# A linear-attention and two-MoE kernel on one core: a new table of steps for the parts, loads and sums of the chunks, with the diagonals and products dealt anew among the engines

## The chip, the cores and the metric

The kernel runs on one core of a Trainium2 chip. The metric is the device time of one execution in microseconds; the kernel before took 535.35 us (median of three runs, 534.69 to 539.89). TensorE (PE) does matmuls and transposes, VectorE (DVE) and GpSimd (POOL) elementwise work, scans and reductions, ScalarE (ACT) activations and copies, and SyncE (SP) issues the DMAs. Each engine works through its own instructions in a fixed order; an instruction waits until what it reads is written and until its buffer is free.

## What is computed

An attention with a decaying state, then a MoE with a clipped gate, then a soft MoE over 32 slots:

```python
for t in range(S):                       # attention, B=4, H=8, S=768, D=48
    cur = np.einsum('bhd,bhe->bhde', u[None] * kt, vt)
    y[:, :, t] = np.einsum('bhd,bhde->bhe', rt, state + cur)
    state = wt[:, :, :, None] * state + np.einsum('bhd,bhe->bhde', kt, vt)
...
h = x @ w_in                             # x: 3072 x 384, w_in: 384 x 2048
g = h * np.clip(h + 3.0, 0.0, 6.0) / 6.0
x = g @ w_out                            # back to 384
...
logits = x @ phi                         # 32 slots, 8 experts
d = softmax(logits, over tokens)
slot_input = d.T @ x
slot_out = relu(slot_input[e] @ w1[e]) @ w2[e]
return softmax(logits, over slots) @ slot_out
```

## The kernel before, in words

**Chunks.** The 3072 tokens are 24 chunks g of 128 tokens, six for each batch. For each chunk two loads are issued on SP: wkr (w, k and r by head pairs, L234) and rkv (r, k and v by tokens, L243). Its parts, with the names used in the tables, are: pw, a scan that gives the running decay e, with a reciprocal and a copy pt on ACT (L250, L252, L254); pv, a second scan (L260); pk and pq, products of k and r with the decays, on DVE or POOL (L263, L270); pg, two squares on ACT that feed a range guard (L267); rk and ru, the products r times k and times u by tokens (L276, L280), and pc, their sum (L284); d0 and d1, two halves of the diagonals of the score matrix, four heads each, on ACT as four activations (L293) or on POOL as one product (L295); sm and sc, the scores and their copy into the masked triangle (L306, L311); kt, the transposed keys (L222, copied at L322); y, the chunk's output (L373, L377, copies L394 and L395); tm and tu, the state's update (L333, L346 to L349).

**Steps.** Three chunks form a block m of 384 tokens. When a block's y is complete, six DMAs on SP rearrange it (L400), and ax splits it into a high and a low part (L419 on ACT; L420 on DVE, or on POOL for blocks 2 and 4). Each block then has 16 steps, 128 in all. Step s does nine matmuls h (L498) into one of three PSUM banks, relu on ACT (L501) and g on DVE (L502, which frees the bank). Two steps later g is transposed: on DVE (L529), whence four DMAs take each group of four steps to DRAM (L518) and one brings it back (L519), or on PE (L222, copied at L540 or L542) at the start and the end. l are the logits' matmuls of four steps (L551). r_logits of a block (rl) splits the logits into two parts (L570 on ACT, L571 on DVE), sums them on PE (L573; L576 and L577 for the last block), takes the minimum (L583, L585) and exponentials (L590, L591, L593); r_back (rb) transposes them (L605), and r_acc (ra) adds the slot inputs into acc (L643, L646). After step 127 follow the experts, from L729 on.

**What sets the order.** The program is written out token by token. START lists the tokens before step 0 by hand. After that every token has a step: a chunk's base step is 16(m-1) plus an entry of YB, each part has a fixed distance from it (pw, pv and rk five steps earlier, sm and sc at it, and so on), and the table LATER shifts single tokens by some steps; PLACES does the same for the loads and splits of the first MoE's weights. Within a step h comes first, then the transposes, l, and the other tokens in order of their entry. A scheduler then places the instructions engine by engine from this sequence, so a shifted token moves its instructions on all engines and its DMAs on SP. The lists RKD, RUD, PKD and PQD name the chunks whose rk, ru, pk or pq run on DVE instead of POOL, DGA the halves whose diagonals run on ACT.

## Time and profile before

| | |
|---|---|
| median of three runs | 535.35 us (534.69 to 539.89) |
| the profiled execution | 535.26 us |
| its span in the trace | 533.5 us, 1.76 us outside it |
| PE busy | 474.5 us, 89% |
| DVE busy | 366.4 us, 69% |
| ACT busy | 237.5 us, 45% |
| POOL busy | 153.0 us, 29% |
| costliest group | h, L498: 1152 matmuls, 232.2 us |
| mean granted TensorE clock | 0.941 |

A row of the timeline gives the start of an instruction or of a run of like ones (x9), its duration, engine, line, operation and tiles; in square brackets stands how long the engine had been idle before it and what ended that idle time. The matmuls of PE overlap, so the duration of one is longer than the distance to the next.

### The profile page before, as it was taken

The page shows a single profiled execution, that of the slowest core. Times are in us where ns is not written, and L with a number is a line of the kernel's source. Part 1 is how long each engine was busy: PE and PEld are TensorE (multiplying, and loading weights), DVE is VectorE, ACT ScalarE, POOL GpSimd, SP SyncE. Part 2 cuts the span into 40 slices and gives each one's busy share as a digit, 9 for nine tenths or more (in the row PEclk, how much of TensorE's full clock was granted, in tenths as well). Part 3 has the DMA queues.
Part 4 walks back from the last instruction along what each step waited for, and adds up shares of the span by engine and source line. Part 5 has one row for each costly group of instructions (what it writes and reads, how often), then busy time and mean ns, then how long its engine had stood idle before and what let it go on. Part 6 is the DMA issues. An engine that isn't in the chain of part 4 may idle for free.

```text
span 533.5 us, 10165 instructions
## 1 busy us (share of the span) xinstructions
PE 474.5 (89%) x3934; PEld 375.0 (70%) x3934; DVE 366.4 (69%) x669; ACT 237.5 (45%) x580; POOL 153.0 (29%) x150
## 2 busy tenths in 40 slices
...
GB/s 297 413 280 123 88 122 183 259 86 70 107 3 109 1 121 109 184 192 279 268 120 249 326 224 145 286 222 197 119 329 199 377 315 336 419 324 270 398 172 232
DMA packets 40263, 114.13 MB, mean 214 GB/s; under 512 B 4464, under 2 KB 22928, under 8 KB 40208
## 3 DMA queue, kind: packets, MB, share of 16 engines
...
q8 instruction: 33, 0.54, 0.4%
...
## 4 chain that ended last, share of the span: by engine, by line
PE 45%; DVE 15%; DMA 9%; ACT 4%; issue 2%; POOL 2%; SPq 1%; POOLq 0%; DVEq 0%; ACTq 0%
PE h L498 22%; DMA rkv<-in_rkv_dram 4%; DMA wkr<-in_wkr_dram 4%; PE lps L551 3%; PE rot L222 3%; PE sides L643 3%; DVE g L502 2%; DVE wkr L260 2%; PE rot L799 2%; DVE e L250 2%; PE rot L373 2%; DVE gsq L529 2%; PE rot L377 2%; PE sides L306 1%; PE po L851 1%
## 5 line engine op out<-in xcount | busy, mean ns | idle before, releaser
L498 PE MATMUL h<-x,wt 128*128 128x384 f32 x1152 | 232.2, 349 | 21.6 <-DVE g L502 11.0
L498 PEld LDWEIGHTS h<-x,wt 128*128 128x128 f32 x1152 | 201.1, 192 | 43.6 <-DVE g L502 15.0
L501 ACT ACTIVATE g<-h,half 128x384 f32<-128x384 f32 x128 | 71.9, 575 | 62.6 <-PE h L498 57.7
L502 DVE SCALAR_TENSOR_TENSOR g<-g,h 128x384 f32<-128x384 f32 x128 | 68.7, 542 | 39.6 <-ACT g L501 36.0
L529 DVE STREAM_TRANSPOSE gsq<-g 128x384 f32<-128x384 f32 x88 | 49.6, 569 | 4.1 <-DMA via<-gsq 2.9
L250 DVE TENSOR_TENSOR_SCAN e<-wkr,d1r 128x516 f32<-128x516 f32 x24 | 32.3, 1351 | 23.2 <-DMA wkr<-in_wkr_dram 23.1
L295 POOL TENSOR_TENSOR att<-cst,cd 128x512 f32<-128x512 f32 x32 | 37.0, 1169 | 27.1 <-DVE cd L284 21.7
L270 POOL TENSOR_TENSOR wkr<-wkr 128x512 f32<-128x512 f32 x18 | 23.9, 1328 | 64.3 <-DVE wkr L260 35.9
L311 DVE COPY_PREDICATED att<-upm,sides 128x512 f32<-128x512 uint32 x48 | 32.1, 721 | 11.3 <-POOL att L295 5.7
L377 PE MATMUL rot<-att,rkv 128*64 128x128 f32 x384 | 32.5, 297 | 7.0 <-DVE att L311 7.0
L260 DVE TENSOR_TENSOR_SCAN wkr<-wkr,d1f 128x516 f32<-128x516 f32 x24 | 35.4, 1475 | 0.1
L377 PEld LDWEIGHTS rot<-att,rkv 128*64 128x64 f32 x384 | 25.0, 147 | 13.9 <-DVE att L311 8.2
L306 PE MATMUL sides<-wkr 64*128 64x128 f32 x384 | 31.6, 302 | 3.2 <-DVE wkr L270 1.2
L263 POOL TENSOR_TENSOR wkr<-wkr,e 128x512 f32<-128x512 f32 x16 | 20.9, 1309 | 44.2 <-DVE e L250 38.2
L306 PEld LDWEIGHTS sides<-wkr 64*128 64x128 f32 x384 | 26.0, 202 | 8.5 <-issue 4.3
L551 PE MATMUL lps<-g,ws 128*32 128x384 f32 x256 | 29.2, 519 | 1.2 <-DVE g L502 1.2
L293 ACT ACTIVATE att<-cst,cd 128x128 f32<-128x128 f32 x64 | 20.3, 393 | 16.5 <-DVE cd L284 16.5
L267 ACT ACTIVATE wkr<-wkr 128x516 f32<-128x516 f32 x24 | 15.2, 633 | 26.1 <-POOL wkr L270 15.6
L349 POOL TENSOR_TENSOR st<-sm,pt 128x192 f32<-128x192 f32 x20 | 13.8, 688 | 43.4 <-DVE sm L348 22.3
L280 POOL TENSOR_TENSOR rkv<-rkv,u_b 128x384 f32<-128x384 f32 x18 | 19.5, 1081 | 21.9 <-DVE rkv L276 9.2
L722 POOL COPY c<-chi 128x128 f32<-128x128 f32 x6 | 2.2, 364 | 78.7 <-DVE chi L720 40.9
L373 PE MATMUL rot<-wkr,st 64*64 64x128 f32 x320 | 24.5, 291 | 0.0
...
## 6 DMA issues: line engine op xcount, KB each, us to landing
...
```

Source lines behind the costliest of these rows:

```text
L250: nc.vector.tensor_tensor_scan(out=flat(e)[:, ::-1], data0=behind.pop(g)[:, ::-1], data1=flat(d1r)[:, ::-1], initial=0.0, op0=ALU.mult, op ...
L260: nc.vector.tensor_tensor_scan(out=fw, data0=fw, data1=fd, initial=0.0, op0=ALU.mult, op1=ALU.add)
L295: nc.gpsimd.tensor_tensor(out=att[g][:, hs, :], in0=ident.unsqueeze(1).to_broadcast([128, 4, C]), in1=cd[g][:, hs].unsqueeze(2).to_broadca ...
L306: nc.tensor.matmul(out=sps[g][:, x, p * C:(p + 1) * C], lhsT=kt_[hs, p, :], rhs=qt_[hs, p, :])
L311: nc.vector.copy_predicated(out=att[g][:, x::2, :], mask=upm.unsqueeze(1).to_broadcast([128, NP, C]), data=ps[:, x].rearrange("p (a t) -> ...
L373: nc.tensor.matmul(out=ps[hs, k * C:(k + 1) * C], lhsT=stl[g][hs, p, :], rhs=qt_[hs, p, :], start=(k == 0), stop=False)
L377: nc.tensor.matmul(out=ps[64 * x:64 * x + 64, k * C:(k + 1) * C], lhsT=vt[:, 2 * p + x, :], rhs=a[:, 2 * p + x, :], start=(first and k == ...
L498: mm = nc.tensor.matmul(out=ps, lhsT=a[:, wp, f % 2, kt * 128:(kt + 1) * 128], rhs=x_[:, xp, kt, :], start=(kt == 0 and i == 0), stop=(kt ...
L501: ra = nc.scalar.activation(out=t, in_=ps, func=ACTF.Relu, scale=1.0 / 6.0, bias=half)
L502: sv = nc.vector.scalar_tensor_tensor(out=t, in0=t, scalar=1.0, in1=ps, op0=ALU.min, op1=ALU.mult)
L529: nc.vector.transpose(out=gsq[m, q][:, :, :, i, :].rearrange("p r j c -> p j r c"), in_=gt[s].rearrange("p (j r c) -> p j r c", j=n, r=4))
L551: mm = nc.tensor.matmul(out=lps[m][32 * i:32 * i + 32, :], lhsT=wsl[q][:, i, :], rhs=gt.pop(NF * m + 4 * q + i), start=(q == 0), stop=(q = ...
```

## The change

Only tables of numbers differ; every part of every chunk is still computed. Of the halves in DGA, seven go from POOL to ACT (chunks 6, 9, 15: first half; 12, 22: second; 10: both) and two come back ((8, 1), (20, 0)). PQD gains pq of chunks 10, 11, 20 and 23 for DVE and loses 13; RKD gains 8 and loses 0 and 14; RUD gains 10 and 20 and loses 8 and 17. YB moves three chunks' base steps by one or two. LATER has other shifts for most tokens, START another order of its tokens, and of PLACES the first four entries change places.

```diff
-RKD = (0, 2, 4, 7, 9, 10, 11, 12, 14, 16, 17, 19, 23)
-RUD = (4, 8, 12, 17, 18, 21)
+RKD = (2, 4, 7, 8, 9, 10, 11, 12, 16, 17, 19, 23)
+RUD = (4, 10, 12, 18, 20, 21)
 PKD = (2, 4, 8, 9, 10, 11, 12, 17)
-PQD = (0, 2, 3, 7, 13, 19)
+PQD = (0, 2, 3, 7, 10, 11, 19, 20, 23)
...
-DGA = ((0, 0), (0, 1), (1, 1), (2, 0), (6, 1), (7, 0), (8, 0), (8, 1), (11, 1), (13, 1), (14, 1), (16, 1), (18, 0), (19, 0), (20, 0), (21, 0))
+DGA = ((0, 0), (0, 1), (1, 1), (2, 0), (6, 0), (6, 1), (7, 0), (8, 0), (9, 0), (10, 0), (10, 1), (11, 1), (12, 1), (13, 1), (14, 1), (15, 0), (16, 1), (18, 0), (19, 0), (21, 0), (22, 1))
...
-YB = ((-5, 3, 5), (0, 4, 8), (-6, -2, 4), (-7, -3, 2), (-6, -2, 2), (-10, -8, -1), (-13, -7, -4))
+YB = ((-5, 3, 3), (0, 4, 8), (-6, -2, 4), (-7, -3, 1), (-6, -1, 2), (-10, -8, -1), (-13, -7, -4))
...
 LATER = {
-    'N7': -5, 'pw4': -1, 'rk7': -4, 'rl0': -1, 'sc8': 1, 'pg10': 1, 'N6': -1, 'tu7': 3, 's10': 2, 'pk13': -2, 'rb6': -1,
...
+    'N7': -5, 'pw4': -3, 'rk7': -2, 'rl0': -1, 'sc8': 2, 'N6': -2, 'tu7': 3, 's10': 2, 'pk13': -2, 'rb6': -1, 's01': 1, 'd18':
```

What this moves is seen in the engines' orders; three places follow, each before and after the change.

The first is ACT at steps 65 to 68. g_3174 is the relu of step 66 in the change (67 before), part is the split of block 3's logits, pt and e belong to the scans of chunks 19 and 20, att is the diagonal of chunk 18. Before:

```order
L254 ACTIVATE pt_3126<-e_3123 128x4
L570 ACTIVATE part_3149<-lps_2694 128x384
L267 ACTIVATE e_3123,guard_96<-e_3123 128x516
L501 ACTIVATE g_3139<-h_3129,half_95 128x384
L501 ACTIVATE g_3174<-h_3164,half_95 128x384
L267 ACTIVATE wkr_3069,guard_96<-wkr_3069 128x516
L293 ACTIVATE att_3180<-cst0_91,cd_3146 128x128 x4
L395 ACTIVATE y_2763<-rot_3098 128x3x128
L254 ACTIVATE pt_3332<-e_3329 128x4
L267 ACTIVATE e_3329,guard_96<-e_3329 128x516
L501 ACTIVATE g_3231<-h_3221,half_95 128x384
```

In the change:

```order
L570 ACTIVATE part_3149<-lps_2810 128x384
L254 ACTIVATE pt_3088<-e_3085 128x4
L501 ACTIVATE g_3174<-h_3164,half_95 128x384
L267 ACTIVATE e_3085,guard_96<-e_3085 128x516
L501 ACTIVATE g_3201<-h_3191,half_95 128x384
L501 ACTIVATE g_3246<-h_3236,half_95 128x384
L267 ACTIVATE wkr_3046,guard_96<-wkr_3046 128x516
L293 ACTIVATE att_3207<-cst0_91,cd_3205 128x128 x2
L590 ACTIVATE e2_3158,zb_3159<-rot_3148,mrun_104 128x384
L591 ACTIVATE al_3160<-mrun_104 128x1
L293 ACTIVATE att_3207<-cst0_91,cd_3205 128x128 x2
```

The split L570 has moved from behind pt of chunk 19 to ahead of it, and the relu of step 68 (g_3231 before, g_3246 now) from behind two squares, the diagonals, a y copy and chunk 20's pt to right behind the relu of step 67.

The second is DVE from g of step 67 (g_3174 before, g_3201 now) on; g of step 68 is g_3231 before and g_3246 now. Before:

```order
L502 SCALAR_TENSOR_TENSOR g_3174<-g_3174,h_3164 128x384
L394 COPY y3_2764<-rot_3098 128x128
L250 SCALAR_TENSOR_TENSOR e_3329<-wkr_3297,d1r_100 128x516
L583 TENSOR_REDUCE mx_3155<-rot_3148 128x1
L529 STREAM_TRANSPOSE gsq_3142<-g_3174 128x3x4x32
L252 RECIPROCAL d1f_99<-e_3329 128x4
L311 COPY_PREDICATED att_3180<-upm_92,sides_3186 128x4x128 x2
L585 TENSOR_TENSOR mrun_104<-mx_3155,mrun_104 128x1
L260 SCALAR_TENSOR_TENSOR wkr_3297<-wkr_3297,d1f_99 128x516
L276 TENSOR_TENSOR rkv_3178<-rkv_3178 128x384
L502 SCALAR_TENSOR_TENSOR g_3231<-g_3231,h_3221 128x384
L593 COPY e2_3158<-rot_3148 32x384
```

In the change:

```order
L502 SCALAR_TENSOR_TENSOR g_3201<-g_3201,h_3191 128x384
L284 TENSOR_REDUCE cd_3205<-rkv_2902 128x8
L585 TENSOR_TENSOR mrun_104<-mx_3155,mrun_104 128x1
L502 SCALAR_TENSOR_TENSOR g_3246<-g_3246,h_3236 128x384
L394 COPY y3_2776<-rot_3117 128x128
L529 STREAM_TRANSPOSE gsq_3177<-g_3201 128x3x4x32
L250 SCALAR_TENSOR_TENSOR e_3332<-wkr_3179,d1r_100 128x516
L529 STREAM_TRANSPOSE gsq_3312<-g_3246 128x3x4x32
L593 COPY e2_3158<-rot_3148 32x384
L600 SCALAR_TENSOR_TENSOR zrun_105<-zrun_105,al_3160,zb_3159 128x1
L311 COPY_PREDICATED att_3207<-upm_92,sides_3213 128x4x128
L252 RECIPROCAL d1f_99<-e_3332 128x4
```

Between the two g stand nine rows before and two now; the y copy, the scan L250 and the rest come behind g of step 68.

The third is PE at steps 126 and 127, where the second MoE's tail begins: L222 are the transposes of g, L551 the logits of four steps, L577 their sum for the last block. Before:

```order
L498 MATMUL h<-x,wt 128x384 x9
L551 MATMUL lps<-g,ws_1040 32x384 x4
L222 MATMUL rot<-cst_91,g 128x128 x3
L498 MATMUL h<-x,wt 128x384 x9
L222 MATMUL rot<-cst_91,g 128x128 x9
L551 MATMUL lps<-g,ws_1214 32x384 x4
L729 MATMUL ctp<-cst_91,c_4699 96x128 x4
L577 MATMUL rot<-part,cst_91 128x384
```

In the change:

```order
L498 MATMUL h<-x,wt 128x384 x11
L222 MATMUL rot<-cst_91,g 128x128 x3
L498 MATMUL h<-x,wt 128x384 x7
L551 MATMUL lps<-g,ws_1051 32x384 x4
L222 MATMUL rot<-cst_91,g 128x128 x6
L551 MATMUL lps<-g,ws_1209 32x384 x4
L729 MATMUL ctp<-cst_91,c_4714 96x128 x4
L222 MATMUL rot<-cst_91,g 128x128 x3
L577 MATMUL rot<-part,cst_91 128x384
```

The logits of steps 120 to 123 (the first L551) have moved behind h of step 127, and those of steps 124 to 127 ahead of the last three transposes.

Told in words: on DVE the sum acc of block 2 (L646) comes one row before the scan of chunk 17 instead of one row behind it; on POOL the first L420 of block 4 comes before ru 16; rk 11 on DVE comes behind g of step 36; rk 14 is now on POOL, right before ru 14. On SP the order of the loads is the same for the first 54 issues; later, three of the four transfers of one gsq tile stand ahead of the y moves of block 5 instead of behind them.

## Rows read from the trace of the kernel before

**Rows 1.** The page's first section: busy us, share, instructions of each engine

```profile
PE 474.5 (89%) x3934; PEld 375.0 (70%) x3934; DVE 366.4 (69%) x669; ACT 237.5 (45%) x580; POOL 153.0 (29%) x150
```

**Rows 2.** Windows: us, busy (instructions) of PE, PEld, DVE, ACT, POOL, PEclk, DMA, GB/s

```profile
0.00:94.00 94.00, 65.85 (x474) 56.77 (x475) 83.74 (x109) 56.49 (x133) 48.93 (x40) 0.82 0.60 217
...
320.00:334.00 14.00, 10.91 (x78) 7.04 (x78) 13.90 (x30) 8.58 (x24) 4.87 (x4) 1.00 0.59 146
...
360.00:374.00 14.00, 11.68 (x70) 9.29 (x69) 12.70 (x27) 8.27 (x23) 7.48 (x7) 1.00 0.75 198
374.00:470.00 96.00, 96.00 (x715) 78.61 (x714) 60.35 (x138) 32.33 (x67) 8.07 (x17) 1.00 0.87 304
470.00:533.50 63.50, 49.32 (x540) 28.26 (x538) 20.05 (x48) 13.19 (x29) 0.65 (x2) 0.90 0.75 272
```

**Rows 3.** Timeline, PE: start, us, engine, line, out<-in, [idle us before <- releaser]

```profile
196.18 2.56 PE L498 MATMUL h<-x,wt 128*128 128x384 f32 x13 [0.51 <-POOL x L420]
...
214.04 0.85 PE L551 MATMUL lps<-g,ws 128*32 128x384 f32 x8 [0.77 <-DVE g L502]
...
268.44 0.62 PE L573 MATMUL rot<-part,sum 128*128 128x384 f32 x2 [1.18 <-ACT y L395]
...
290.39 1.16 PE L306 MATMUL sides<-wkr 64*128 64x128 f32 x16 [0.98 <-DVE acc L646]
...
295.62 0.97 PE L498 MATMUL h<-x,wt 128*128 128x384 f32 x4 [0.59 <-POOL x L420]
...
311.35 0.44 PE L573 MATMUL rot<-part,sum 128*128 128x384 f32 x1 [1.08 <-ACT part L570]
...
324.29 1.86 PE L498 MATMUL h<-x,wt 128*128 128x384 f32 x9 [2.52 <-DVE g L502]
...
329.23 1.84 PE L498 MATMUL h<-x,wt 128*128 128x384 f32 x9 [0.57 <-DVE g L502]
...
364.96 1.86 PE L498 MATMUL h<-x,wt 128*128 128x384 f32 x9 [1.62 <-DVE g L502]
...
472.24 0.52 PE L222 MATMUL rot<-cst,g 128*128 128x128 f32 x3 [0.88 <-DVE g L502]
```

**Rows 4.** Lines L295, L270, L276: duration ns (min/median/max), first and last start

```profile
L295 POOL TENSOR_TENSOR att<-cst,cd x32: 1033/1040/1959, 23.9 to 397.3; 128x512 f32<-128x512 f32 x32
...
L270 POOL TENSOR_TENSOR wkr<-wkr x18: 1181/1193/2101, 16.4 to 370.2; 128x512 f32<-128x512 f32 x18
...
L270 DVE TENSOR_TENSOR wkr<-wkr x6: 676/692/1489, 12.1 to 315.3; 128x512 f32<-128x512 f32 x6
...
L276 DVE TENSOR_TENSOR rkv<-rkv x13: 525/551/1283, 5.0 to 393.9; 128x384 f32<-128x384 f32 x13
L276 POOL TENSOR_TENSOR rkv<-rkv x11: 991/1006/1307, 20.7 to 369.2; 128x384 f32<-128x384 f32 x11
```

**Rows 5.** Timeline: a half of the diagonals on ACT, rk 11 on DVE

```profile
266.65 1.28 ACT L293 ACTIVATE att<-cst,cd 128x128 f32<-128x128 f32 x4 [2.87 <-DVE cd L284]
...
212.81 0.71 DVE L276 TENSOR_TENSOR rkv<-rkv 128x384 f32<-128x384 f32 x1 [0.58 <-DMA rkv<-in_rkv_dram]
```

**Rows 6.** Timeline: scans of chunks 17 and 19 on DVE, two diagonals on POOL

```profile
288.46 1.23 DVE L250 TENSOR_TENSOR_SCAN e<-wkr,d1r 128x516 f32<-128x516 f32 x1 [5.23 <-DMA wkr<-in_wkr_dram]
...
308.59 2.09 DVE L250 TENSOR_TENSOR_SCAN e<-wkr,d1r 128x516 f32<-128x516 f32 x1 [1.18 <-DMA wkr<-in_wkr_dram]
...
307.55 2.04 POOL L295 TENSOR_TENSOR att<-cst,cd 128x512 f32<-128x512 f32 x2
```

**Rows 7.** Timeline, ACT and DVE: what stands before g 68, and g 69

```profile
321.90 0.56 ACT L501 ACTIVATE g<-h,half 128x384 f32<-128x384 f32 x1
...
318.02 0.28 DVE L394 COPY y<-rot 128x128 f32<-128x128 f32 x1
...
323.69 0.54 DVE L502 SCALAR_TENSOR_TENSOR g<-g,h 128x384 f32<-128x384 f32 x1
...
325.84 0.56 DVE L502 SCALAR_TENSOR_TENSOR g<-g,h 128x384 f32<-128x384 f32 x1
```

More of the change, by code (lines that the diff above doesn't have):

```diff
@@ L1130 @@
 WARM = [17, 4, 3, 0]
-YB = ((-5, 3, 5), (0, 4, 8), (-6, -2, 4), (-7, -3, 2), (-6, -2, 2), (-10, -8, -1), (-13, -7, -4))
+YB = ((-5, 3, 3), (0, 4, 8), (-6, -2, 4), (-7, -3, 1), (-6, -1, 2), (-10, -8, -1), (-13, -7, -4))
 PLACES = {
-    'W2': 2, 'W3': 3, 'W1': 1, 'W0': 0, 'W4': 1, 'V0': 4, 'V1': 5, 'W5': 4, 'V2': 2, 'V3': 3, 'V4': 5, 'V5': 4, 'W6': 3, 'V6':
+    'W1': 1, 'W0': 0, 'W3': 3, 'W2': 2, 'W4': 1, 'V0': 4, 'V1': 5, 'W5': 4, 'V2': 2, 'V3': 3, 'V4': 5, 'V5': 4, 'W6': 3, 'V6':
     3, 'V7': 4, 'W7': 5
```

6 lines of the change are left out of this document (3 added, 3 removed), and 54 rows, old and new, of the table LATER.

## The prediction

> **What bounds the kernel now.** I read the page's busy line first: TensorE (PE) is busy 474.5 of 533.5 us, VectorE (DVE) 366.4, ScalarE (ACT) 237.5, GpSimd (POOL) 153.0 [rows 1]. So PE is the bound, 59 us of its time are idle, and a change that adds and removes no matmul can only move those 59 us. The table by stretches [rows 2] says where they lie. In the first 94 us PE is busy 65.85 us and DVE 83.74: 28 idle us belong to the start. In 374 to 470 us PE is busy 96.00 of 96.00, so whatever is gained or lost before it is carried to the end whole. In 320 to 334 us PE has 3.09 us idle while DVE is busy 13.90 of 14.00; in 360 to 374 us it has 2.32 idle and DVE 12.70. The granted clock reads 1.00 in both, so nothing is to be had from the clock there. Then I read PE's timeline for the stalls themselves, each with its releaser [rows 3]; those of the middle and one in the tail are what the new order can reach. The reader is to see that no stall waits on a load directly: each waits for a DVE, ACT or POOL result, and that instruction stood behind another one in its engine's fixed order. A step's h uses one of three PSUM banks, so h of step s+3 waits for g (L502) of step s; that is the releaser of the largest stalls.
>
> **What the change does to engines.** The list DGA gains seven halves of the diagonals and loses two: 5 more on ACT. A half costs POOL 1.04 us (median) and ACT four activations, 1.28 us together [rows 4, 5]. So ACT gets 6.4 us, POOL loses 5.2. Four pq go from POOL (median 1.19) to DVE (0.69) and one comes back; two rk go to POOL and one comes from it (1.01 on POOL, 0.55 on DVE [rows 4]), and of ru as many go as come (taken as rk's price). Sum for POOL: -5.2 - 3 x 1.19 + 1.01 = about -8 us of 153; for DVE 3 x 0.69 - 0.55 = +1.5 us of 366. Neither total bounds anything: ACT is idle 296 us and POOL 380 [rows 1]. I cost the totals at 0; if their cover were gone in the stretches where DVE is full, a pq on DVE costs its length, 0.69 to 1.49 [rows 4].
>
> **What the new order does to the stalls.** The first 28 steps (0 to about 93 us) keep their order but for some prep steps, and rk 0 on POOL instead of DVE falls into time in which both still wait for loads: 0. Later, stall by stall:
>
> - *Block 2, 214.04, 0.77 us.* l waits for g 35, which stands behind rk 11 on DVE; rk 11 waited for its load until 212.81 [rows 5]. Now rk 11 stands behind g 36. -0.7.
> - *POOL's x products.* h waits for L420 twice, 0.51 us at 196.18 and 0.59 at 295.62 [rows 3]. In both cases a pq or ru stood ahead of L420 on POOL. pq 11 leaves POOL, and the first L420 of block 4 now comes before ru 16. -0.3 for the first; the second is in the next item.
> - *290.39 and 295.62, 0.98 + 0.59.* The scores of a chunk wait for acc (L646), which stands behind the scan of chunk 17 on DVE, and that scan waited 5.23 us for its load [rows 6]. acc now stands ahead of the scan. 1.57 in all; I take -1.3, since ACT's L419 before L420 keeps a few tenths.
> - *311.35, 1.08.* The next sum waits for part (L570) on ACT, behind pt 19, which waits for the scan at 308.59 [rows 3, 6]. L570 now stands ahead of pt 19. L571, the second part, stays behind the scan, but the second matmul on it was already later (the row at 311.35 is one matmul of the two). -0.8.
> - *324.29 and 329.23, 2.52 + 0.57.* h 71 waits for g 68. Its relu ran at 321.90 on ACT and g 68 at 323.69 on DVE, behind nine rows, the first at 318.02 [rows 7]: 5.67 us of work. Now relu 68 follows relu 67 and g 68 follows g 67 but for two short reductions, so g 68 is done before PE wants h 71 and the 2.52 us go. The work is only put later: before g 69 now stand the y copy, the scan of chunk 20, two transposes, L593, L600, L311, a reciprocal and rk 19, some 6 us. With g 68 at about 318.4, g 69 comes at about 324.9 (325.84 before [rows 7]), so h 72 becomes the stall, about 0.9 us earlier than before; g 70 then comes about 1.5 to 2 us earlier. -1.7 of 3.09, with -0.9 and -3.09 as ends.
> - *364.96, 1.62, and the rest of that stretch's 2.32 [rows 2, 3].* The same swap for relu 80 and g 80, but pq 23 is new on DVE ahead of g 83, and the scan of chunk 22 now stands before g 81. -0.5, ends 0 and -2.3.
> - *268.44, 1.18.* L573, the sum of the logits of a block, waits for a y copy on ACT behind a diagonal, behind pc 14, ru 14, rk 14 and a load. rk 14 moves from DVE to POOL ahead of ru 14: 1.01 instead of 0.55 [rows 4]. +0.5.
> - *Tail, 472.24, 0.88.* The transposes of g 127 wait for g 127, behind a copy of the tile on DVE. Now g 127 is ahead of that copy, the four logit matmuls of the third weight group come after h 127, and the last four come before the transposes. Eight L551 took 0.85, so h 127 ends 0.43 earlier; with the stall of 0.88 and the 0.5 of the three transposes taken from in front of the last logits, part (L576) is about 1.6 earlier. L577, which needs it, now stands behind those three transposes, 0.5. -1.1.
>
> Sum: -0.7 - 0.3 - 1.3 - 0.8 - 1.7 - 0.5 + 0.5 - 1.1 = -5.9. Every other step was shuffled as well, and such shuffles leave stalls of 0.3 to 0.7 behind, as [rows 3] has them; pq 23 in a full stretch is half a new one (0.4). I add +0.4: -5.5. The profiled execution took 535.26 us (0.09 under the median of the three), so the forecast is 529.8 us.
>
> **Rivals.**
>
> *The full DVE keeps its time.* In 320 to 334 and 360 to 374 us DVE has 0.1 and 1.3 us free. If those two stretches are set by the amount of DVE work and not by its order, e and f, the two items on g 68 and g 80, give nothing, and of pq 20 and pq 23 (0.69 to 1.49 each) about 1 us comes on top. For: [rows 2]. Against: after 334 us PE does not stall for 26 us, so DVE's lag is absorbed. Time: 529.8 + 2.2 + about 1 = 533.0 us.
>
> *Slower: stops at loads.* DVE and ACT run in order; one that stops at a load not yet landed holds every relu and g behind it. The scan of chunk 17 stopped 5.23 us and that of 19 1.18 [rows 6]. On the SyncE queue three of the four transfers of a gsq tile now come ahead of the six y moves of block 5, where all four stood behind them; the load of the next chunk waits behind these too. If an issue slips by 3 us at each of four such stops between 210 and 370 us and half is not covered, 6 us are lost, and with only the tail's and one other gain (-2) kept the time is 539 to 541 us. It decides when DVE's idle time behind the wkr loads grows by more than about 8 us. For: stops exist; against: before such stops cost PE at most 1 us each [rows 3].
>
> *Freed POOL makes DVE faster.* The scan at 308.59 took 2.09 us beside two POOL diagonals (2.04 from 307.55), while the scan at 288.46, with POOL idle, took 1.23 [rows 6]. With 8 us less of POOL work, DVE instructions are held up less, above all in the start, where DVE sets the pace. If five such hold-ups of 0.5 to 0.9 vanish on the path, the time is 529.8 - 3 = 527 us. The Trainium skill (SBUF — State Buffer, "SBUF: two separate sides") states that VectorE and GpSimd share a port pair as an exclusive lock that one holds for a whole instruction, VectorE also when it has two SBUF inputs and the GpSimd instruction reads SBUF. The trace agrees at 308.59 (0.86 us added, less than one diagonal of 1.04). The same rule speaks against the three more pq on DVE, which could each be held by a POOL instruction, as the longest DVE pq so far, 1.49, may have been.
>
> **How the numbers follow.** A measurement of this kernel can tell about 1%, 5.35 us, from no change, so faster means below 530.0. The forecast (527.5 to 531.7) has 0.62, and it straddles that line: I put 0.42 below and 0.20 above. The full DVE has 0.21, all of it same. The freed POOL has 0.08, faster; the stops at loads have 0.09, slower. So faster 0.50, same 0.41, slower 0.09. The bounds: if every stall named vanished, -0.77 - 0.51 - 1.57 - 1.08 - 3.09 - 2.32 - 1.18 - 1.6 = -12.1, 523; that asks for no new stall anywhere. The range leaves out the slower case and the outer half of the two ends: 526 to 535.
>
> **What would show it.** Right: PE stalls at h 71, at the scores after L646, at L573 of the third sum and at the transposes of g 127 gone or under 0.3 us; h 72 or h 73 the first stall of block 4, at under 1.5 us; PE idle in 94 to 470 us down from 16.7 (59.0 less 28.15 at the start and 14.18 after 470 [rows 2]) to about 12; 0 to 94 us unchanged within 0.6 us; POOL near 145 us. Wrong: a new stall of over 1 us in 160 to 320 us behind a load, or a start that moved by more than 1 us, since I cost it at nothing.

## The result and the profile after

The changed kernel took 530.79 us in the median of 20 runs (526.51 to 533.93), the kernel before 535.13 us in as many (533.07 to 540.08) beside it. The ratio is 0.9894 with a 95% interval of 0.9871 to 0.9918: 1.06% faster, 5.7 us of 535.13; the two medians alone differ by 4.3 us (0.8%). Ratios here and below are taken from the executions within 1.5% of their kernel's fastest, medians from all. The prediction was 529.8 us, range 526 to 535, with faster by over 1% as its likeliest class. The profiled execution of the change took 527.37 us, below its median (before: 535.26), so its rows flatter the change by some 3 us, and the experiments below have to say which part of the difference is the change's.

The page's busy line and the windows of the change, in the same columns as [rows 1, 2]:

```profile
PE 472.2 (90%) x3934; PEld 372.6 (71%) x3934; DVE 366.6 (70%) x671; ACT 242.9 (46%) x600; POOL 147.3 (28%) x143
```

```profile
0.00:94.00 94.00, 65.75 (x476) 55.73 (x476) 83.80 (x108) 55.27 (x131) 49.00 (x41) 0.82 0.58 211
...
320.00:334.00 14.00, 12.91 (x119) 9.20 (x119) 12.85 (x28) 7.67 (x22) 4.29 (x4) 1.00 0.78 225
...
360.00:374.00 14.00, 12.93 (x81) 10.45 (x80) 12.53 (x29) 7.16 (x19) 3.56 (x3) 1.00 0.56 151
...
470.00:525.50 55.50, 42.96 (x500) 23.89 (x498) 16.92 (x40) 9.47 (x21) 0.65 (x2) 0.91 0.74 262
```

ACT has 5.4 us more and POOL 5.7 less, DVE is as it was. The start is unchanged. From 94 to 470 us PE is idle 525.5 - 472.2 - 28.25 - 12.54 = 12.5 us, where before it was 16.7. The stretches do not cover quite the same work, since everything is earlier by then, so the comparison from here on goes by landmarks in the program. **Stretch A** runs from the first logits of steps 8 to 11 to those of steps 72 to 75, **stretch B** from there to the last logits; PE's idle time is the length less PE's busy time. Windows of the kernel before: start, A and B:

```profile
0.00:141.31 141.31, 110.56 (x807) 94.76 (x807) 115.24 (x156) 84.87 (x209) 64.96 (x54) 0.83 0.53 187
141.31:348.95 207.64, 195.90 (x1701) 154.66 (x1703) 149.66 (x289) 94.15 (x244) 68.11 (x68) 0.99 0.56 174
348.95:472.69 123.74, 120.55 (x906) 98.71 (x899) 82.48 (x181) 46.32 (x101) 19.24 (x26) 1.00 0.84 286
```

The same of the change:

```profile
0.00:141.89 141.89, 109.69 (x807) 93.32 (x808) 116.04 (x157) 85.59 (x213) 64.41 (x54) 0.83 0.52 186
141.89:340.34 198.45, 192.92 (x1684) 153.48 (x1687) 146.81 (x287) 96.94 (x256) 61.18 (x61) 1.00 0.57 181
340.34:465.10 124.76, 122.69 (x919) 99.31 (x911) 84.37 (x183) 47.76 (x105) 21.02 (x27) 1.00 0.84 282
```

The last logits come 7.59 us earlier (472.69 to 465.10). PE's idle time up to them falls from 45.69 to 39.80 us, by 5.89; the other 1.70 us are less busy time, of which three transposes now behind the last logits are about 0.4. Of the idle time, A gives 6.2 us (11.74 to 5.53), B 1.1 (3.19 to 2.07), and the start takes 1.4 (30.75 to 32.20). So the gain was made before the change's 340 us, as predicted. The start's idle time is the least telling of the three: it goes up and down with the granted clock (30.02 us at 0.81 in e8 below, 33.89 at 0.85 in e1), while the length of the start stays within 140.0 and 143.6 us in all profiles.

PE's timeline of the change, the stalls of 0.45 us and more between 160 and 370 us, with the idle time and its releaser in brackets as in [rows 3]:

```profile
168.04 0.55 PE L222 MATMUL rot<-cst,g 128*128 128x128 f32 x3 [1.01 <-DVE sm L348]
...
270.46 1.85 PE L498 MATMUL h<-x,wt 128*128 128x384 f32 x9 [1.05 <-DVE g L502]
...
289.23 0.67 PE L333 MATMUL rot<-rkv,knat 128*64 128x48 f32 x16 [1.32 <-ACT knat L322]
...
321.35 1.67 PE L498 MATMUL h<-x,wt 128*128 128x384 f32 x8 [0.47 <-DVE g L502]
...
358.62 0.44 PE L573 MATMUL rot<-part,sum 128*128 128x384 f32 x1 [0.45 <-ACT part L570]
...
359.60 1.84 PE L498 MATMUL h<-x,wt 128*128 128x384 f32 x9 [0.54 <-DVE g L502]
...
362.11 3.42 PE L498 MATMUL h<-x,wt 128*128 128x384 f32 x18 [0.48 <-DVE g L502]
...
366.90 3.41 PE L498 MATMUL h<-x,wt 128*128 128x384 f32 x18 [0.59 <-DVE g L502]
```

Of the ten stalls of [rows 3] three have a remnant: 0.47 us at h 73 for those at 324.29 and 329.23, and the four from 358 to 367 us, 2.06 together, for that at 364.96 and its stretch. The others are gone in this execution; e12 below shows another. Three new ones of over 1 us stand at 168, 270 and 289 us. On DVE the place of [rows 6] has changed too, the scan of chunk 17 and the sum acc that now precedes it:

```profile
281.78 0.75 DVE L646 SCALAR_TENSOR_TENSOR acc<-acc,al,sides 128x512 f32<-128x512 f32 x1 [0.66 <-PE sides L643]
284.09 1.23 DVE L250 TENSOR_TENSOR_SCAN e<-wkr,d1r 128x516 f32<-128x516 f32 x1 [1.56 <-DMA wkr<-in_wkr_dram]
```

DVE stopped 1.56 us at this load instead of 5.23 [rows 6]. The load was issued at 279.32 us instead of 281.44, and landed faster: the DMA issues of 276 to 290 us, kernel before, and of 276 to 288 us, change (KB, us from issue to landing at the end):

```profile
wkr<-in_wkr_dram SPq DMA_DIRECT2D x1, 770.0 KB, 7.0
```

```profile
wkr<-in_wkr_dram SPq DMA_DIRECT2D x1, 770.0 KB, 4.7
```

### The profile page after: what moved, and what is told of

It is laid out like the page before. It is cut to its first block, busy times and chain, and to the rows that moved or that the text cites. A ratio compares the mean times of both kernels' runs of the same rounds, so it can differ in the third digit from the quotient of the medians.

```text
span 525.5 us, 10173 instructions
## 1 busy us (share of the span) xinstructions
PE 472.2 (90%) x3934; PEld 372.6 (71%) x3934; DVE 366.6 (70%) x671; ACT 242.9 (46%) x600; POOL 147.3 (28%) x143
## 4 chain that ended last, share of the span: by engine, by line
PE 54%; DVE 10%; DMA 8%; SPq 2%; ACT 2%; issue 2%; POOL 0%; DVEq 0%; ACTq 0%; POOLq 0%
PE h L498 26%; DMA wkr<-in_wkr_dram 4%; PE rot L222 4%; PE lps L551 3%; PE sides L643 3%; PE sides L306 3%; PE rot L373 2%; PE rot L377 2%; PE rot L799 2%; DMA rkv<-in_rkv_dram 2%; DMA y<-y 1%; PE so L822 1%; DVE e L250 1%; PE po L851 1%; PE rot L485 1%
## 5 line engine op out<-in xcount | busy, mean ns | idle before, releaser
L250 DVE TENSOR_TENSOR_SCAN e<-wkr,d1r 128x516 f32<-128x516 f32 x24 | 31.2, 1302 | 20.4 <-DMA wkr<-in_wkr_dram 20.3
L295 POOL TENSOR_TENSOR att<-cst,cd 128x512 f32<-128x512 f32 x27 | 33.1, 1234 | 29.3 <-DVE cd L284 27.6
L260 DVE TENSOR_TENSOR_SCAN wkr<-wkr,d1f 128x516 f32<-128x516 f32 x24 | 35.3, 1470 | 0.1
L293 ACT ACTIVATE att<-cst,cd 128x128 f32<-128x128 f32 x84 | 26.6, 393 | 18.5 <-DVE cd L284 18.5
L263 POOL TENSOR_TENSOR wkr<-wkr,e 128x512 f32<-128x512 f32 x16 | 21.9, 1372 | 44.2 <-DVE e L250 33.7
L270 POOL TENSOR_TENSOR wkr<-wkr 128x512 f32<-128x512 f32 x15 | 19.8, 1320 | 42.5 <-DVE wkr L260 40.8
L551 PE MATMUL lps<-g,ws 128*32 128x384 f32 x256 | 29.4, 509 | 0.4 <-DVE g L502 0.4
L349 POOL TENSOR_TENSOR st<-sm,pt 128x192 f32<-128x192 f32 x20 | 12.7, 634 | 55.5 <-DVE sm L348 45.1
L395 ACT ACTIVATE y<-rot 128x384 f32<-128x384 f32 x21 | 10.2, 488 | 35.4 <-DVE y L394 35.4
```

The costliest lines, as they stand in the source:

```text
L250: nc.vector.tensor_tensor_scan(out=flat(e)[:, ::-1], data0=behind.pop(g)[:, ::-1], data1=flat(d1r)[:, ::-1], initial=0.0, op0=ALU.mult, op ...
L260: nc.vector.tensor_tensor_scan(out=fw, data0=fw, data1=fd, initial=0.0, op0=ALU.mult, op1=ALU.add)
L295: nc.gpsimd.tensor_tensor(out=att[g][:, hs, :], in0=ident.unsqueeze(1).to_broadcast([128, 4, C]), in1=cd[g][:, hs].unsqueeze(2).to_broadca ...
L551: mm = nc.tensor.matmul(out=lps[m][32 * i:32 * i + 32, :], lhsT=wsl[q][:, i, :], rhs=gt.pop(NF * m + 4 * q + i), start=(q == 0), stop=(q = ...
```

## The experiments

Twelve runs, each timed against the kernel before on the same chip. The theory on trial was that of the prediction: named rows of the order, moved past stops, remove named stalls, and the totals of the engines cost nothing. Its rivals were that the full DVE keeps its time, and that something else, a load's place or the four lists, carries the gain. The table has every result; idle and busy times of PE are read as above from windows, the last two columns from the span's start to the last logits. Kernels built on the kernel before stand above, kernels built on the change below.

| run | median us | ratio to before, 95% | idle A | idle B | idle, all | busy, all |
|---|---|---|---|---|---|---|
| before (first profile) | 535.13 | | 11.74 | 3.19 | 45.69 | 427.00 |
| e1_tail | 536.16 | 0.9985 [0.9957, 1.0014] | 12.12 | 1.81 | 47.82 | 426.00 |
| e2_b7 | 537.97 | 0.9999 [0.9957, 1.0042] | 11.48 | 3.57 | 45.24 | 430.56 |
| e3_b5 | 539.40 | 1.0004 [0.9966, 1.0042] | 12.03 | 3.86 | 46.53 | 427.44 |
| e7_early | 539.44 | 1.0056 [1.0016, 1.0096] | 10.27 | 3.21 | 47.27 | 430.51 |
| e4_lists | 535.05 | 0.9948 [0.9912, 0.9984] | | |  |  |
| change (first profile) | 530.79 | 0.9894 [0.9871, 0.9918] | 5.53 | 2.07 | 39.80 | 425.30 |
| e12_change | 530.33 | 0.9877 [0.9828, 0.9927] | 7.34 | 2.38 | 39.88 | 430.69 |
| e5_nolate | 529.78 | 0.9920 [0.9882, 0.9959] | 5.34 | 3.12 | 40.27 | 424.30 |
| e6_tables | 541.40 | 1.0132 [1.0080, 1.0183] | 11.64 | 2.53 | 46.57 | 435.06 |
| e9_dga | 541.55 | 1.0102 [1.0066, 1.0137] | 13.00 | 2.32 | 45.59 | 430.07 |
| e10_pqrkru | 532.98 | 0.9931 [0.9890, 0.9971] | 6.91 | 1.29 | 41.25 | 427.34 |
| e8_load17 | 535.68 | 1.0020 [0.9979, 1.0060] | 5.44 | 4.63 | 40.09 | 433.37 |
| e11_tailed | 527.84 | 0.9847 [0.9801, 0.9894] | 7.66 | 3.34 | 43.96 | 421.47 |

The kernel before had medians of 535.13, 536.87, 535.55 and 535.91 us in the four sessions; the ratios are taken within one. No run varied YB, START or PLACES apart from the rest. In the profiles the idle time and the busy time move separately: e6 and e7, which are slower than the kernel before, have no more idle time in A than it has, but 5.7 and 7.3 us more busy time there, at a granted clock of 0.96 against 0.99.

**e1_tail: the tail alone, on the kernel before.**

```diff
 LATER = {
-    ... 'l26': 3, ... 'l30': 4, ... 'l25': 7, ...
+    ... 'l26': 1, ... 'l30': 2, ... 'l25': 4, ... 'l24': 2, 'l29': 5
```

> The kernel before with only the shifts of l 24 to l 31 from the change (five entries of LATER); on PE the logits of steps 120 to 123 then stand behind h 127 and the last logits ahead of the last three transposes, as in the change. Stall by stall: the 0.88 us stall at 472 goes and the last logits come earlier, L577 1.1 us earlier, -0.8 to -1.2 us in all. Rival, the tail is set by its weight loads: no change within 0.3 us, with a new idle time of PE behind a load after 475 us.

PE's timeline of e1_tail where the second MoE's tail begins:

```profile
472.23 0.85 PE L551 MATMUL lps<-g,ws 128*32 128x384 f32 x8
473.02 0.87 PE L222 MATMUL rot<-cst,g 128*128 128x128 f32 x6
473.82 0.85 PE L551 MATMUL lps<-g,ws 128*32 128x384 f32 x8
...
475.08 0.49 PE L222 MATMUL rot<-cst,g 128*128 128x128 f32 x3
475.41 0.85 PE L577 MATMUL rot<-part,cst 128*128 128x384 f32 x2
```

The stall of 0.88 us before the transposes [rows 3] is gone, and from the logits of steps 112 to 115 to the last ones 24.35 us pass instead of 25.47: 1.12 us, as the tail's term had it (1.1). The change itself has 24.34 there. The time alone cannot show 1.1 us: the ratio's interval holds both nothing and the gain.

**e2_b7: the shifts of chunks 21 to 23 alone** (36 entries of LATER), that is the swap of relu 80 and g 80.

```diff
-    ... 'N23': -2, ... 'tu21': 4, ... 'L23': -6, ... 'ru21': -1, ...
+    ... 'N23': -4, ... 'tu21': 3, ... 'L23': -7, ... 'ru21': -4, ... 'ru22': -3, ... 'pq23': 1, ...
```

> The kernel before with only the shifts of chunks 21 to 23 from the change; relu 80 and g 80 then stand two and five rows behind those of step 79, instead of six and nine. Stall by stall: the stall of 1.62 us at h 83 goes, part of it comes back at h 84 to h 87: -0.5 us (0 to -2.3). Rival, the full DVE keeps its time: 0 within 0.2 us, since DVE is busy 12.7 of 14.0 us there and the same work stands in the stretch.

The stalls of this stretch, PE's timeline of e2_b7:

```profile
369.88 1.85 PE L498 MATMUL h<-x,wt 128*128 128x384 f32 x9 [2.19 <-DVE g L502]
```

With 0.49 us more at 372.40 that is 2.68 us, where the kernel before has 2.32 in all of 360 to 374 us [rows 2]. The swap alone removes nothing; in this place the rival of the full DVE had it right.

**e3_b5: the shifts of chunks 15 to 17 alone** (31 entries), which bring relu 68 and g 68 forward, but not all the way: five rows stand between g 67 and g 68, where the change has two.

```diff
-    ... 'L17': -3, ... 'kt17': 6, ... 'L16': -1, ... 'pq16': 1, ... 'ru16': 1, ... 'tu17': -2, ...
+    ... 'L17': -2, ... 'kt17': 7, ... 'L16': -5, ... 'pq16': 3, ... 'ru16': -2, ... 'tu17': -6, ...
```

> The kernel before with only the shifts of chunks 15 to 17 from the change; relu 68 then follows relu 67 by two rows and g 68 g 67 by six, instead of six and ten, and L570 of block 3 stands ahead of pt 19. Stall by stall: of the stalls at 311 (1.08), 324 (2.52) and 329 (0.57) some 2.5 us go, and up to 0.6 more at 290 and 295: -2 to -3 us. Rival, the full DVE keeps its time: only the 0.8 us of L570, and h 72 to h 75 stall by what h 71 no longer does.

PE's timeline of e3_b5, then the window of 316 to 332 us:

```profile
320.74 1.86 PE L498 MATMUL h<-x,wt 128*128 128x384 f32 x9 [0.64 <-DVE g L502]
...
324.44 0.40 PE L605 MATMUL rot<-cst,e 64*128 64x64 f32 x3 [1.06 <-DVE e L593]
...
327.05 3.25 PE L498 MATMUL h<-x,wt 128*128 128x384 f32 x9 [1.63 <-DVE g L502]
```

```profile
316.00:332.00 16.00, 12.66 (x87) 10.55 (x90) 15.90 (x29) 9.10 (x27) 7.17 (x7) 0.89 0.56 166
```

The stalls sum to 3.33 us against 3.09 before [rows 3]: they have moved to other waiters. DVE is busy 15.90 of 16.00 us, and it still stopped 5.34 us at the load of chunk 17. The stall of h 71 fell from 2.52 to 0.64 us and h 72 took 1.63, the form that the prediction gave to what is put later; the sum did not shrink. Since neither the order nor the stop is that of the change, this run doesn't part the two.

**e4_lists: the four lists RKD, RUD, PQD and DGA alone.**

```diff
-DGA = (... (6, 1), (7, 0), (8, 0), (8, 1), (11, 1), ..., (20, 0), (21, 0))
+DGA = (... (6, 0), (6, 1), (7, 0), (8, 0), (9, 0), (10, 0), (10, 1), (11, 1), ..., (21, 0), (22, 1))
...
```

> The kernel before with only the four lists RKD, RUD, PQD and DGA of the change, all steps as before. The scheduler moves some rows for it: relu 68 comes two rows behind relu 67 and L570 ahead of pt 19. Stall by stall: the totals cost nothing, those two moves give -2 to -3 us. Freed POOL makes DVE faster: -3 us more, with DVE's mean scan and product shorter and PE's idle time in the first 94 us down by over 1 us. Full DVE: -0.8 us or less.

Only its time is used, since its profile is of an execution of 540.40 us, 1% over its median. The ratio is 0.9948, some 0.5% faster, the interval just off 1. That is 2.8 us, what was expected of the two rows that the scheduler moves; it says nothing against totals at 0.

**e7_early: the shifts of the chunks below 12, of the sums of blocks 0 and 1 and of l below 10 alone** (93 entries; such a part of the table is no single line, so one entry stands for it).

```diff
-    ... 'Q10': 3, ... 'L3': -1, ...
+    ... 'Q10': 9, ... 'L3': -5, ...
```

> The kernel before with the shifts of the early tokens alone (chunks below 12, the sums of blocks 0 and 1, l below 10). Stall by stall: of the stalls at 153, 173, 196 and 213 us (0.4, 0.5, 0.5, 0.8) about 1.5 us go, and the start adds 0 to 1.5 as in the change's trace, nothing later: 0 to -1.5 us. If the early shifts also bring the later stops at loads forward, the stalls at h 63 to h 75 shrink by over 1 us as well.

0.56% slower. The stalls at 196, 214, 268, 290 and 295 us are gone here, without the lists and without the late shifts. Others come instead: 1.61 us at 152.77, 1.76 at 246.60, 1.27 at 274.92 and 1.06 at 277.83, so that A's idle time falls by no more than 1.5 us (10.27 against 11.74); most of what its profile loses is PE's busy time (table). What e7 keeps is the stall of h 71. DVE's scan of chunk 17, then PE's h 71, in e7:

```profile
292.42 1.23 DVE L250 TENSOR_TENSOR_SCAN e<-wkr,d1r 128x516 f32<-128x516 f32 x1 [2.21 <-DMA wkr<-in_wkr_dram]
```

```profile
328.66 2.47 PE L498 MATMUL h<-x,wt 128*128 128x384 f32 x9 [2.90 <-DVE g L502]
```

The stop at the load is 2.21 us instead of 5.23, and h 71 still waits 2.90 us for g 68 (at 328.06), which has the same rows ahead of it as in the kernel before.

**e5_nolate: the change, with the shifts of chunks from 15 on, of the block sums from 3 on and of l from 14 on as before** (121 entries).

```diff
-    ... 'pq16': 3, ... 'L16': -5, ... 'tu17': -6, ... 'l29': 5, ...
+    ... 'pq16': 1, ... 'L16': -1, ... 'tu17': -2, ...
```

> The change with the shifts of the late tokens as before (chunks 15 to 23, the block sums from block 3 on, l from 14 on); the lists and everything earlier as in the change. relu 68 and g 68 keep the change's places, relu 80 and the tail have those of before. If the gain of h 63 to h 75 comes from what stands earlier, it stays: PE idle between the logits of steps 56 and 72 as in the change within 1 us, 1.1 us lost in the tail, nothing at relu 80: ratio about 0.992. If the late shifts make it, 3 us more are lost there: ratio about 0.998.

The gain stays: ratio 0.992, and A has 5.34 us idle, like the change (5.53). B loses the tail's 1.1. The stalls at h 71 and h 73 stay away as well: 0.46 us at 319.52 is what is left there. As was expected, the order at g 68 is still that of the change, although the shifts of chunks 15 to 17 are those of before. DVE's timeline of e5, from g 67 to g 68:

```profile
310.13 0.54 DVE L502 SCALAR_TENSOR_TENSOR g<-g,h 128x384 f32<-128x384 f32 x1
310.59 0.54 DVE L284 TENSOR_REDUCE cd<-rkv 128x8 f32<-128x384 f32 x1
311.05 0.15 DVE L585 TENSOR_TENSOR mrun<-mx,mrun 128x1 f32<-128x1 f32 x1
311.12 0.55 DVE L502 SCALAR_TENSOR_TENSOR g<-g,h 128x384 f32<-128x384 f32 x1
```

So the lists and the earlier shifts bring this order about, and e5 can't say what the time would be without it.

**e6_tables: the change with the four lists as before.**

```diff
-RKD = (2, 4, 7, 8, 9, 10, 11, 12, 16, 17, 19, 23)
+RKD = (0, 2, 4, 7, 9, 10, 11, 12, 14, 16, 17, 19, 23)
-PQD = (0, 2, 3, 7, 10, 11, 19, 20, 23)
+PQD = (0, 2, 3, 7, 13, 19)
...
```

> The change with the four lists as before, all steps as in the change. relu 68 then stands four rows behind relu 67 and g 68 eight behind g 67. If the totals cost nothing: the stalls of 173 to 295 us gone as in the change, about half of the gain at h 71 to h 75 lost, ratio about 0.992. Freed POOL: DVE's work grows slower again, 3 us lost, ratio about 0.995 to 0.998.

541.4 us, 1.3% slower than before: the shifts without the lists are a loss, with them a gain. PE's idle time up to the last logits (46.57 us) is 0.9 us above that of the kernel before: the gain in idle time is gone, and the rest of the loss in this profile is busy time (435.06 us against 427.00). One of its stalls shows how a POOL product can hold up PE. PE's timeline of e6_tables, then DVE's, then POOL's, all near 264 us:

```profile
265.99 1.09 PE L373 MATMUL rot<-wkr,st 64*64 64x128 f32 x16 [1.27 <-POOL st L349]
```

```profile
263.60 2.04 DVE L260 TENSOR_TENSOR_SCAN wkr<-wkr,d1f 128x516 f32<-128x516 f32 x1
```

```profile
263.36 1.19 POOL L263 TENSOR_TENSOR wkr<-wkr,e 128x512 f32<-128x512 f32 x1 [12.42 <-DVE e L250]
264.51 1.43 POOL L349 TENSOR_TENSOR st<-sm,pt 128x192 f32<-128x192 f32 x1
```

and the lines of L349 and L260 in e6_tables (ns, min/median/max, first and last start):

```profile
L349 POOL TENSOR_TENSOR st<-sm,pt x20: 505/507/1432, 20.4 to 407.9; 128x192 f32<-128x192 f32 x20
```

```profile
L260 DVE TENSOR_TENSOR_SCAN wkr<-wkr,d1f x24: 1191/1226/2183, 11.2 to 375.8; 128x516 f32<-128x516 f32 x24
```

Beside a product on POOL the scan took 2.04 us where its median is 1.23, and the state update L349, which began while the scan ran, took 1.43 where its median is 0.51; PE waited 1.27 us for it. The Trainium skill (SBUF — State Buffer, "SBUF: two separate sides") says that VectorE and GpSimd hold a shared port pair one at a time, each for a whole instruction; the trace agrees, with 0.81 us added on the one and 0.92 on the other. The product here, L263, is a pk, and PKD is the same in both kernels, so this shows a hold-up and not what the changed lists are worth.

**e9_dga and e10_pqrkru: which of the lists.** e9 is the change with DGA alone as before, e10 the change with PQD, RKD and RUD as before.

```diff
 # e9_dga
-DGA = (... (6, 0), ..., (9, 0), (10, 0), (10, 1), ..., (12, 1), ..., (15, 0), ..., (22, 1))
+DGA = (... (6, 1), ..., (8, 1), (11, 1), ..., (20, 0), (21, 0))
 # e10_pqrkru
-PQD = (0, 2, 3, 7, 10, 11, 19, 20, 23)
+PQD = (0, 2, 3, 7, 13, 19)
...
```

> The change with only the list of diagonals DGA as before: five halves go back from ACT to POOL, all steps as in the change. The scheduler then puts relu 68 four rows behind relu 67 and g 68 eight behind g 67. If POOL's share is what makes the steps work (its diagonals and products ahead of the state's update, which PE waits for): ratio 1.003 or more, with stalls of PE behind the state's product on POOL. If the totals cost nothing, as the prediction had it: 0.990 to 0.995.

> The change with the lists PQD, RKD and RUD as before (pq, rk, ru), the diagonals as in the change. g 68 then stands 13 rows behind g 67. If the five halves are what matters: 0.995 or less. If every list has to fit the steps: 1.000 or more, with the stall at h 71 back at over 1.5 us.

e9 is 1.0% slower than before, about 2.2% (11 us) behind the change of the same session; e10 keeps most of the gain (0.9931, 0.5% behind the change, which is within the intervals). So with these shifts it is the diagonals on ACT that matter, together with the rows that the scheduler moves for them, and the three lists of products matter little. In the profiles e9 has 5.7 us more idle time than the change, all of the gain; its profiled execution (537.83 us) is the fastest of its eight, so the rest of the 11 us is not seen there. PE's timeline of e9:

```profile
243.34 0.85 PE L551 MATMUL lps<-g,ws 128*32 128x384 f32 x8 [2.18 <-DVE g L502]
...
293.31 0.67 PE L333 MATMUL rot<-rkv,knat 128*64 128x48 f32 x16 [2.13 <-ACT knat L322]
```

and of its DVE, with the page's busy line:

```profile
289.93 1.23 DVE L250 TENSOR_TENSOR_SCAN e<-wkr,d1r 128x516 f32<-128x516 f32 x1 [3.86 <-DMA wkr<-in_wkr_dram]
```

```profile
PE 477.5 (89%) x3934; PEld 377.5 (70%) x3934; DVE 371.8 (69%) x671; ACT 237.2 (44%) x580; POOL 152.2 (28%) x148
```

DVE is busy 5.2 us longer than in the change for the same 671 instructions. The scans are not where it lies (L260 has 35.5 us in e9, 35.3 in the change); it is spread over many lines. The stop at chunk 17 is back to 3.86 us, and A's idle time to 13.00. But e9 is not only a matter of POOL's and DVE's time: the scheduler places other rows as well when the diagonals go back, among them those around g 68. How much each of the two is worth stays open. In e10 one old stall comes back, and A still ends with 6.91. DVE's g 68 in e10 (with g 69 merged to it), then PE's h 71:

```profile
319.01 1.01 DVE L502 SCALAR_TENSOR_TENSOR g<-g,h 128x384 f32<-128x384 f32 x2
```

```profile
319.61 6.12 PE L498 MATMUL h<-x,wt 128*128 128x384 f32 x18 [2.94 <-DVE g L502]
```

g 67 ran at 310.91 and 13 instructions stand between the two, 7.6 us of work, though DVE had stopped only 1.34 us at the load of chunk 17.

**e8_load17: the change, with the load wkr of chunk 17 issued behind the y moves**, at 285.93 us instead of 279.32.

```diff
-    ... 'L17': -2, ...
+    ... 'L17': -1, ...
-PIN = {'L5': 'h1', 'L6': 'h0'}
+PIN = {'L5': 'h1', 'L6': 'h0', 'L17': 'y14'}
```

> The change with the load of chunk 17's w, k, r issued behind the six y moves of block 4 instead of ahead of them, some 5 us later. The scheduler puts the scan of chunk 17 seven rows behind acc for it; relu 68 and g 68 still come two and one rows behind those of step 67. If DVE's pile of work behind a late load makes the stalls of h 71 to h 73: PE idle between the logits of steps 56 and 72 grows by 1.5 to 4 us. If the order of g 68 alone decides: less than 0.7 us.

The whole gain is lost (1.002), but not where I looked for it. DVE stopped 2.30 us at another load (rkv, L276 at 285.17) and 1.12 us at the scan, which now ran at 290.38, and A's idle time did not grow (5.44). Two larger stalls came later, in PE's timeline of e8:

```profile
346.50 0.66 PE L222 MATMUL rot<-cst,wkr 128*128 128x128 f32 x4 [1.26 <-ACT y L395]
...
365.71 0.69 PE L573 MATMUL rot<-part,sum 128*128 128x384 f32 x1 [2.85 <-ACT part L570]
```

and in the window of its stretch B, where the granted clock is 0.97 and PE's busy time 125.51 us, against 1.00 and 122.69 for 919 instructions in the change:

```profile
343.32:473.46 130.14, 125.51 (x920) 101.77 (x912) 84.59 (x186) 46.94 (x105) 21.49 (x28) 0.97 0.80 275
```

So B has 2.6 us more idle time than in the change's first profile and 2.8 us more busy time at the lower clock. Against the change's second profile (e12) it is 2.3 and 1.6, and that profile has a stall of 1.86 us at the place of the one of 2.85, without the edit. Up to the last logits PE's idle time is 40.09 us, as in the change. That one load 6.6 us later, with the rows that the scheduler moves along with it, takes back the gain is shown by the twelve times; by what way is not.

**e11_tailed: the change without the late shifts, but with those of the tail** (e5_nolate with the five entries of e1_tail).

```diff
-    ... 'pq16': 3, ... 'L16': -5, ... 'tu17': -6, ...
+    ... 'pq16': 1, ... 'L16': -1, ... 'tu17': -2, ... 'l24': 2, 'l29': 5
```

> The change without the late shifts (as the run that undid them) but with those of l 24 to l 31: the tail as in the change, relu 80 as before. That run had 39.06 us of PE idle up to the last logits, 0.88 of them the tail's stall; so 38.2 here against 38.6 of the change, and a time 0.1 to 0.2% below the change if the clock is the same; equal to it if executions differ by more than that.

527.84 us, ratio 0.9847 [0.9801, 0.9894]: the lowest median of all, below the change's 530.33 in the same session. The two intervals overlap, so that it beats the kernel before is shown, that it beats the change is not. Its profile has 43.96 us of idle time where 38.2 was expected, 4.2 more than the change's, and 3.8 us less busy time than the change's first profile, and the two profiled executions are 0.61 us apart (527.98 and 527.37). The expectation for the idle time failed.

**e12_change: the change once more**, on the same chip right beside e9, e10 and e11, with a second profile.

> The change itself, on the same chip as the three runs beside it: ratio 0.987 to 0.992 as measured before, PE idle up to the last logits 38 to 39 us.

The same program, profiled at 533.12 us instead of 527.37. Windows of the change's first profile, then of this one:

```profile
360.00:380.00 20.00, 18.93 (x156) 13.93 (x154) 14.70 (x35) 7.16 (x19) 4.07 (x4) 1.00 0.56 146
```

```profile
360.00:380.00 20.00, 17.62 (x97) 14.81 (x96) 18.37 (x39) 11.73 (x31) 5.93 (x5) 0.91 0.67 176
```

Summed over the start, A and B, PE's idle time up to the last logits is 39.88 us here and 39.80 there; its busy time is 430.69 and 425.30. The clock reads 1.00 (2.4 GHz) in this stretch of the first profile; 0.91 in the second means that part of it was granted 1.2 GHz. So of the 5.75 us between two executions of one program 5.4 are busy time at a lower granted clock (0.931 and 0.945 as means), and a saving of 5.8 to 5.9 us of idle time is seen twice: 45.69 before, 39.80 and 39.88 after. That the two sums agree so well is partly chance: A has 1.8 us more idle time in the second profile and the start 2.0 less, so that A and B together save 7.3 us in the one and 5.2 in the other.

Nor do single stalls all repeat. Those at 196, 214, 324 and 472 us are gone in both profiles, and 0.47 us at h 73 and 1.09 at 292.20 (1.32 at 289.23 in the first) are left in both. But 0.87 us at 268.43 and 1.86 at 363.94 stand in the second alone, and the third sum of logits waits again, now for the second part, L571 on DVE:

```profile
310.66 0.44 PE L573 MATMUL rot<-part,sum 128*128 128x384 f32 x1 [0.97 <-DVE part L571]
```

## Why the prediction was right, point by point

The time (529.8 against 530.79) and the size of the gain (5.5 us forecast; 5.7 by the ratio, 4.3 by the medians, 5.9 in PE's idle time) came out. The mechanism, rows moved past the stops that PE's stalls went back to, came out for the tail, for 196 and 214 and, as far as e7 and e10 show it, for the largest item. That the sum is so near is in part luck: misses of up to 1 us in both directions offset each other, and the step that cost the totals of the engines at nothing is spoken against by e9.

| step | forecast | measured |
|---|---|---|
| totals of the engines | 0 | diagonals, with the rows moved for them: 11 us with these shifts |
| start, 0 to 94 us | 0 | -0.10 busy PE: none |
| 214.04 | -0.7 | -0.77 |
| 196.18 | -0.3 | -0.51 |
| 290.39, 295.62 | -1.3 | -1.57, but +1.32 at 289.23: -0.25 |
| 311.35 | -0.8 | -1.08 |
| 324.29, 329.23 | -1.7 | -2.62 |
| 364.96 and its stretch | -0.5 | -0.26 |
| 268.44 | +0.5 | -1.18, but +1.05 at 270.46: -0.13 |
| tail | -1.1 | -1.12 (e1) |
| further new stalls | +0.4 | +1.01 at 168.04 |

The measured column is read from the first profile. Without its first row it sums to -5.7 us, but it is a selection: stalls of 0.51 to 0.69 us at 144 and 173 us went as well, 0.30 of the 1.32 and 0.26 of the 1.01 us stood there before (at 292.77 and 169.47), and the start has 1.4 us more idle time. The sum is no check of the total.

- **The tail, 214, 196 and 311.** The tail went as worked out and is shown by an experiment of its own (e1). The stalls at 214 and 196 are gone in both profiles of the change and in e7. That at 311 is gone in the first profile; in the second 0.97 us is left, for L571 on DVE, which the prediction had left behind the scan.
- **290 and 295: the stall changed its place.** acc ahead of the scan did free the scores. But the same wait, a y move that lands late, stood behind it: L419 on ACT waited for it and the keys' copy L322 came behind. ACT's timeline of the change:

```profile
288.17 0.52 ACT L419 ACTIVATE x<-y 128x384 fp32r<-128x384 f32 x1 [1.24 <-DMA y<-y]
288.60 0.58 ACT L322 ACTIVATE knat<-rot 128x512 f32<-128x512 f32 x1
```

  The term allowed "a few tenths" for L419; L419 waited 1.24 us, and PE 1.32. The term was mis-sized since I followed L419 to its own reader and not to the row behind it.
- **324 and 329: the order is what the runs bear out, and the term was too small.** The prediction moved 5.67 us of work behind g 68 and kept a stall at h 72. In the change 0.47 us is left, at h 73. The kernels with two rows between g 67 and g 68 (the change twice, e5, e11) all have 0.46 to 0.47 us left there. With the rows of before the stall stays although the stop at chunk 17's load is short: e7 has 2.90 us after a stop of 2.21, and e10, with 13 instructions between, 2.94 after one of 1.34. e3, with five, moved it without making it smaller. DVE is no less full in the change: from g 66 to PE's wait at h 73 it is busy 12.81 of 12.90 us (308.4 to 321.3), in the kernel before, from g 66 to the end of the wait of h 71, 9.37 of 9.40 (314.9 to 324.3). So it is not that DVE has less to do. Why nothing of the expected stall came back at h 72 stays open, and no run gives the change this one order alone.
- **364: the order alone gives nothing** (e2), and in the change 0.26 us; e5 and e11, with the order of before, have 2.19 and 2.02 us in their largest stall there.
- **268: the price was wrong in sign.** rk 14 on POOL did not lengthen the wait; a stall of 1.05 us stands at h 59 instead, released by a g on DVE. In the second profile 0.87 us is left at L573, for L348 on DVE.
- **The totals cost nothing: this is the step that the runs speak against.** The prediction said that ACT's and POOL's idle time covers them. With the shifts of the change, taking the diagonals back to POOL costs 2.2% (e9 against e12). Part of that can be the rows that the scheduler moves for it, g 68 among them (eight instructions stand between it and g 67 in e9), so the price of the totals alone isn't known; e4 fits totals at 0. An average idle share of 70% on POOL says nothing about the moments in which a product there stands before a reader, or holds up a DVE instruction, as e6 shows at 264 us. The change is no sum of its parts: shifts alone lose (e6: +1.3%; the early ones, e7: +0.6%), lists alone give half, both together 1.06 to 1.2%.
- **The rivals.** The full DVE was right at g 80 (e2) and for the sum of e3, wrong for the change, where DVE is as full at g 68 and PE does not wait. Stops at loads: in e8 one load issued 6.6 us later undoes the gain, which is this rival's cause if not its way, but in the change these stops became shorter (DVE's idle time before L250 for loads 20.3 us against 23.1). Freed POOL: DVE's busy total did not fall (366.4 [rows 1] and 366.6), nor did the scans L260 (35.4 and 35.3 us), so as a shortening of DVE it is hardly seen between before and change, though by the prediction's count the total should have grown by 1.5 us, the scans L250 have 31.2 us against 32.3, and e9 has 5.2 us more. It stays a small part that is not ruled out.

- **The signs that it named.** PE idle from 94 to 470 us was to be about 12 us: 12.5. Start unchanged: yes. POOL near 145 us: 147.3, 5.7 us less where 8 were forecast. L573 of the third sum under 0.3 us: in the first profile, not in the second (0.97). The first stall of block 4 at h 72 or h 73, under 1.5 us: h 73, 0.47. A new stall of over 1 us behind a load between 160 and 320 us was to speak against it: none behind a load of a chunk, but that of 289.23 goes back to a y move.

**What stays open.** The length of the stop at chunk 17's load goes with the idle time of A in most profiles: 3.9 to 5.3 us before, in e1, e2, e3, e6 and e9, with 11.5 to 13.0 us idle; 1.0 to 1.6 in the change (twice), e5, e8, e10 and e11, with 5.3 to 7.7. e7, with 2.21 and 10.27, lies between. It is a correlation; no run changed that stop and nothing else, and at h 71 e7 and e10 speak for the order instead. How the 6.2 us of A divide among the moved rows is not measured, since no run moves one of them alone. Nor is it settled why that load landed in 4.7 us instead of 7.0, how e9's loss divides between POOL's time and the scheduler's other order, by what way e8 loses its time, and whether the lower clock in A in the profiles of e6 and e7 is theirs or that of one execution.
